# Converting float64 weights in place, without GpSimd, with later turns of gathered tokens and one conditional part

## The chip, the cores and the metric

The kernel runs on one core of a Trainium2 chip. Its engines are named as in the profile: PE (TensorE; PEld is its weight load), DVE (VectorE), ACT (ScalarE), POOL (GpSimd) and SP (SyncE, which here issues loads and stores). The metric is the device time of one execution in microseconds; of several runs the median is given.

## The reference, cut to what matters

Three parts follow each other: attention over chunks of 32 tokens with 8 memory keys, a dense feed-forward layer over 3072 tokens (model width 512, hidden 2048), and a routed layer in which each token goes to one of 8 experts (hidden 1024).

```python
for c in range(S // 32):                      # chunk attention, 4 x 8 heads, 768 tokens
    scores = q_c @ concat(mem_k, k_ctx).T / 8
    a = exp(scores - max); a = a / (sum + 1e-9)
    out[chunk] = a @ concat(mem_v, v_ctx)
h = x @ w_in                                  # dense layer, 512 -> 2048 -> 512
x = (h * sigmoid(h)) @ w_out
logits = x @ w_gate + modality_bias[modality_id]
e = argmax(logits); gate = softmax(logits)[e]
for each expert: out[mask] = gate[mask] * (relu(x[mask] @ w1[e]) @ w2[e])
```

The dense weights w_in and w_out reach the kernel as float64: two 32-bit words for each number.

## The kernel before

**Stages.** The 3072 tokens are taken in 8 blocks of 384. A block is four attention sub-blocks of 96 tokens, then 16 dense steps f of 128 hidden units, then the routing of its tokens. After the eight blocks come the expert tiles of 384 gathered tokens (two early ones, e0 and e1, six large ones, b0 to b5) and one small tile of 128 (s0). Block 0's dense steps run while the 16 pairs of weights (step f of w_in and of w_out, half 0 and half 1) are still being loaded and converted; later blocks use the converted pairs, which stay on chip.

**Products.** A product with full precision is three products of a reduced type, fp32r: high x high, high x low and low x high. So each weight is held as a high and a low part (tiles wh and wl), and so are the activations (xh and xl, gh and gl). `prod_h` (lines 469 to 475) makes the hidden units (tile hp), `prod_y` (477 to 482) the outputs (tile yp). Between them stand a tanh on ACT, `tanh_1` on DVE (508), a rounding copy on ACT (513, gh) and a subtraction on DVE (514, gl).

**Conversion** (lines 410 to 467) turns the two words of a float64 into a float32. The upper word has sign, exponent and the top of the mantissa, the lower word the rest. For both halves of a step:

- `load` (420, 422): two transfers of 512 KB, w_in as four pieces of 256 words per partition, w_out as 1024 words in one piece;
- `scale_down` (ACT, 429; DVE for step 0): the upper word, read as a float, times 2^-112, into tile wm;
- `shift` (DVE, 433): wm of both halves shifted left by 3, one instruction over 1024 words;
- `sign` (DVE, 437): the sign bit of the upper word is merged into wm;
- `rest` (ACT, 444, or DVE, 442, for the steps in `D_T1`): the lower word times 2^-29, into tile wt;
- `whole` (POOL, 448): wm = wm + wt as integers;
- `high` (ACT, 451): wh = wm rounded to fp32r;
- `low` (455): wl = wm - wh, on DVE for half 1 and on POOL for half 0.

**Attention.** Of a sub-block, `minima` (DVE, 355) reads the scores, `exps` (ACT, 362) makes the exponentials, `sums` (DVE, 367, 368) their reciprocal sums, `norm` (POOL, 373) scales two halves of four heads; then PE turns them (377), a copy (380) and the product with the values (385) follow, and the split into xh and xl (388, 391).

**Experts.** For each tile `ids` finds the tokens, `gather` (POOL, 843) fetches 128 rows from HBM by indirect DMA (tile xg), `turn` (PE, 849) transposes them into PSUM (xp), and ACT and DVE split them (852 and on). `put` (POOL, 1008) scatters results. The routing may need more tiles than the static ones: a seventh and further large tile, or a second and further small one. Each has a conditional part at the end (1037 to 1046), which loads a count into a register on all engines and skips the part where the count is not above 6 or 1.

**What sets the order.** All instructions are units of a planner (`Plan`): each has an engine, a cost in ns, a lag behind it (`extra`, the time of a transfer), the units that it waits for and its tiles. A list scheduler puts them in one static order per engine; nothing is reordered at run time. For a gather the lag is `DMA_LAG + 800` = 2700 ns; for a weight load 1900 ns. The load of step f waits for the last unit that reads the lower words of step f - 3. A list `first` fixes the order of the first loads.

```python
U(f"ga{x}", "Pool", 1040, lambda t=t: gather(t), [f"id{nm}/{gi}"], [f"xg{x}", f"gi{nm}"], extra=DMA_LAG + 800, **F)
U(f"tx{x}", "PE", 430, lambda t=t: turn(t), [f"ga{x}"], [f"xg{x}", f"xp{x}"], **F)
```

## Time and profile before

| | |
|---|---|
| median of 3 runs | 1007.29 us (1005.69 to 1008.43) |
| profiled execution | 1009.41 us |
| its span | 1007.6 us |
| mean granted TensorE clock, as a share of full | 0.972 |
| PE busy | 947.0 us (94%) |
| PEld busy | 834.9 us (83%) |
| DVE busy | 668.8 us (66%) |
| ACT busy | 442.4 us (44%) |
| POOL busy | 208.6 us (21%) |

Busy times are unions over one profiled execution, from the first to the last instruction; the execution's own time has 1.8 us more than the span. A share over the whole span is a mean over stages, so the stages are to be looked at one by one.

### The profile page before, as it was taken

What the parts mean: (1) busy time and instruction counts of PE and PEld (TensorE: products, weight loads), DVE (VectorE), ACT (ScalarE), POOL (GpSimd) and SP (SyncE); (2) the same over time, 40 slices, a digit from 0 to 9 for tenths busy, and PEclk for the clock granted to TensorE, in tenths of its full rate; (3) what the DMA queues carried; (4) which work ended last, traced back from release to release, by engine and by line L of the source; (5) the groups of instructions that cost most, each with busy time, mean ns of one, the idle gap of its engine ahead of it and who ended that gap; (6) DMA issues with size and microseconds to landing.
All of it is one profiled execution on the core that took longest, in us unless ns stands there. A gap on an engine that the chain in (4) does not pass through costs nothing. (4 is left out here: it accounts for less than half of the span.)

```text
span 1007.6 us, 16028 instructions
## 1 busy us (share of the span) xinstructions
PE 947.0 (94%) x5516; PEld 834.9 (83%) x5516; DVE 668.8 (66%) x1959; ACT 442.4 (44%) x1201; POOL 208.6 (21%) x174
## 2 busy tenths in 40 slices
PE   6687789999999999999999999999999999999994
...
GB/s 299 276 92 157 91 121 62 99 11 111 91 31 89 83 60 62 99 72 61 100 72 61 82 32 45 40 159 187 32 212 206 141 173 172 150 152 209 126 44 45
DMA packets 102402, 111.00 MB, mean 110 GB/s; under 512 B 22591, under 2 KB 76639, under 8 KB 102304
## 3 DMA queue, kind: packets, MB, share of 16 engines
...
q14 instruction: 51, 0.42, 0.1%
HBM read 97.20 MB, written 12.85 MB: 109 GB/s over the span
## 5 line engine op out<-in xcount | busy, mean ns | idle before, releaser
L373 POOL TENSOR_TENSOR pt<-pt,rs 96x512 f32<-96x512 f32 x64 | 80.6, 1278 | 416.3 <-DVE rs L368 340.4
L362 ACT ACTIVATE pt<-pt,mn 96x128 f32<-96x128 f32 x256 | 99.6, 391 | 27.9 <-DVE mn L355 27.7
L448 POOL TENSOR_TENSOR wm<-wm,wt 128x512 int32<-128x512 int32 x32 | 50.8, 1600 | 19.4 <-DVE wm L437 13.3
L362 ACT ACTIVATION_READ_ACCUMULATOR pt<-pt,mn 96x1 f32 x256 | 48.3, 189 | 0.0
L385 PE MATMUL pv<-px,v 128*64 128x96 f32 x512 | 30.8, 266 | 4.0 <-DVE mn L355 2.6
L385 PEld LDWEIGHTS pv<-px,v 128*64 128x64 f32 x512 | 24.6, 147 | 12.0 <-DVE mn L355 4.7
L455 POOL TENSOR_TENSOR wl<-wm,wh 128x512 fp32r<-128x512 f32 x16 | 24.7, 1544 | 4.5 <-ACT wh L451 4.5
L391 DVE TENSOR_TENSOR xl<-pv,xh 128x384 fp32r<-128x384 f32 x32 | 17.5, 547 | 11.8 <-ACT xh L388 11.8
L451 ACT CAST wh<-wm 128x512 fp32r<-128x512 f32 x32 | 19.6, 617 | 9.6 <-POOL wm L448 9.6
L388 ACT CAST xh<-pv 128x384 fp32r<-128x384 f32 x32 | 15.1, 473 | 18.4 <-PE pv L385 18.4
L455 DVE TENSOR_TENSOR wl<-wm,wh 128x512 fp32r<-128x512 f32 x16 | 21.1, 1321 | 1.3 <-ACT wh L451 1.3
L355 DVE DVE_READ_ACCUMULATOR2_ANT mn<- 96x1 f32 x256 | 20.1, 79 | 0.0
L433 DVE TENSOR_SCALAR wm<-wm 128x1024 int32<-128x1024 int32 x16 | 19.1, 1194 | 0.1
L843 POOL DMA_INDIRECT xge0.0_6891<-yd,gie x1 | 1.2, 1171 | 76.2 <-DMA rawxe0.1_6861<-in_moe_w_dram 76.2
L545 DVE DVE_READ_ACCUMULATOR2_ANT lg<- 128x1 f32 x192 | 15.5, 81 | 0.0
L367 DVE TENSOR_SCALAR rs<-sm 96x8 f32<-96x8 f32 x32 | 6.7, 210 | 1.8 <-ACT pt L362 1.8
L585 DVE TENSOR_SCALAR ya<-ya,rg 128x512 f32<-128x512 f32 x16 | 7.6, 481 | 0.0
L368 DVE RECIPROCAL rs<-rs 96x8 f32<-96x8 f32 x32 | 6.4, 199 | 1.1
L627 DVE TENSOR_SCALAR rej<-rows,rj 128x24 f32<-128x24 f32 x24 | 7.1, 294 | 0.0
L1008 POOL DMA_INDIRECT out_dram<-bye0.0_7456,sxe x1 | 1.0, 1024 | 28.4 <-ACT bye0.0_7456 L1005 28.4
L562 DVE TENSOR_SCALAR rw<-rd 128x24 f32<-128x24 f32 x8 | 5.6, 701 | 0.1
L474 PE MATMUL hp0.0_447<-xl,wh 128*128 128x384 f32 x4 | 1.6, 563 | 4.3 <-DVE xl L391 4.3
...
## 6 DMA issues: line engine op xcount, KB each, us to landing
...
wd0.0_100<-in_moe_w_in_dram SPq DMA_DIRECT2D x1, 512.0 KB
wd0.1_102<-in_moe_w_out_dram SPq DMA_DIRECT2D x1, 512.0 KB
wd1.0_152<-in_moe_w_in_dram SPq DMA_DIRECT2D x1, 512.0 KB
```

What stands on the lines that cost most here:

```text
L355: dve.tensor_tensor_reduce(out=T[f"pt{n}"][:, h, :], in0=T[f"sc{n}.{i // 2}"][:, h % 4, :], in1=mask, scale=-scale, scalar=3.0e38, op0=ALU ...
L362: act.activation(out=pt[:, h, :], in_=pt[:, h, :], func=AF.Exp, bias=T[f"mn{n}"][:, h:h + 1], scale=-1.0, accum_out=T[f"sm{n}"][:, h:h + 1])
L373: pool.tensor_tensor(out=pt[:, half, :], in0=pt[:, half, :], in1=bc(T[f"rs{n}"][:, half], [QB, 4, P]), op=ALU.mult)
L385: pe.matmul(T[f"pv{n}"][r:r + 64, h // 2, :], T[f"v{n}"][:, D * h:D * h + D], T[f"px{n}"][:, 4 * (h % 2) + h // 2, :], start=True, stop=True)
L388: act.copy(out=T[f"xh{j}"][:, :, cols], in_=T[f"pv{n}"])
L391: dve.tensor_tensor(out=T[f"xl{j}"][:, :, cols], in0=T[f"pv{n}"], in1=T[f"xh{j}"][:, :, cols].bitcast(F32), op=ALU.subtract)
L433: dve.tensor_scalar(out=mi, in0=mi, scalar1=3, scalar2=None, op0=ALU.logical_shift_left)
L448: pool.tensor_tensor(out=mi, in0=mi, in1=T[f"wt{f}"][:, i], op=ALU.add)
L451: (dve.tensor_copy if f in D_CH else act.copy)(out=T[f"wh{f}"][:, i], in_=T[f"wm{f}"][:, i])
L455: e.tensor_tensor(out=T[f"wl{f}"][:, i], in0=T[f"wm{f}"][:, i], in1=T[f"wh{f}"][:, i].bitcast(F32), op=ALU.subtract)
L545: dve.tensor_tensor_reduce(out=part(products), in0=part(y_at[t]), in1=T[f"wg{j}.{e // 2}"][:, e % 2], scale=1.0, scalar=0.0, op0=ALU.mult, ...
L585: dve.tensor_scalar(out=y, in0=y, scalar1=T[f"rg{j}"][:, t:t + 1], scalar2=None, op0=ALU.mult)
```

## The change

It has three parts, and a fourth that follows from the first.

1. *The conversion is done in place, and POOL has no part in it.* Tiles wm and wt are gone. The lower word is scaled where it stands (line 422 on DVE with a minimum of 7 for the steps in `D_T`; line 424 on ACT with a factor just under 2^-29), the sign is merged into it (428, DVE), the upper word is scaled where it stands (432, ACT), one instruction shifts the upper word left by 3 and merges the lower word into it by a bitwise or (436, DVE), the high part is rounded from it (439, ACT) and the low part is subtracted (442, DVE, both halves). So the integer addition becomes an or, and the shift has no instruction of its own.
2. *Gathers have a lag of 6500 ns in the plan* in the place of 2700.
3. *One conditional part* covers further large and further small tiles. The planning writes one number, the sum of two comparisons, in the place of two counts; the small list is planned behind the large one.
4. *Loads.* The host lays w_in and w_out out so that each half of a step is one piece of 4 KB per partition. Each half is a unit of its own, waits for the merge of its half three steps back, and has a place of its own in `first`.

```diff
+GATHER_LAG = 6500.0
...
-D_T1 = range(0, 16, 3)
-D_LO = [(f, 1) for f in range(16)]
-D_C1 = (0,)
-D_CH = ()
+D_T = range(0, 16, 3)
...
     def conversion(f):
         for i in range(2):
             T.new(f"wd{f}.{i}", "w", [P, DM, 2], I32)
-        T.new(f"wm{f}", "w", [P, 2, DM])
-        T.new(f"wt{f}", "w", [P, 2, DM], I32)
         T.new(f"wh{f}", "w", [P, 2, DM], F32R)
         T.new(f"wl{f}", "w", [P, 2, DM], F32R)
-        wd = [f"wd{f}.0", f"wd{f}.1"]
-
-        def load():
-            sp.dma_start(
-                out=T[wd[0]].rearrange("p (c f) w -> p c (f w)", c=KD), in_=w_in[:, f * P:f * P + P].bitcast(I32).rearrange("(c p) x -> p c x", p=P))
-            sp.dma_start(out=T[wd[1]].rearrange("p f w -> p (f w)"), in_=w_out[f * P:f * P + P, :].bitcast(I32))
-
-        def scale_down(i):
-            m, x = T[f"wm{f}"][:, i], T[wd[i]][:, :, 1].bitcast(F32)
-            if f in D_C1:
-                dve.tensor_scalar(out=m, in0=x, scalar1=2.0 ** -112, scalar2=None, op0=ALU.mult)
+
+        def load(i):
+            sp.dma_start(out=T[f"wd{f}.{i}"].rearrange("p f w -> p (f w)"), in_=(w_in, w_out)[i][f].bitcast(I32))
+
+        def rest(i):
+            x = T[f"wd{f}.{i}"][:, :, 0]
+            if f in D_T:
+                dve.tensor_scalar(out=x, in0=x.bitcast(U32), scalar1=2.0 ** -29, scalar2=7.0, op0=ALU.mult, op1=ALU.min)
             else:
-                act.activation(out=m, in_=x, func=AF.Copy, scale=2.0 ** -112)
-
-        def shift():
-            mi = T[f"wm{f}"].bitcast(I32)
-            dve.tensor_scalar(out=mi, in0=mi, scalar1=3, scalar2=None, op0=ALU.logical_shift_left)
+                act.activation(out=x, in_=x.bitcast(U32), func=AF.Copy, scale=7.49 * 2.0 ** -32)
 
         def sign(i):
-            mi = T[f"wm{f}"][:, i].bitcast(I32)
-            dve.scalar_tensor_tensor(out=mi, in0=T[wd[i]][:, :, 1], scalar=-2 ** 31, in1=mi, op0=ALU.bitwise_and, op1=ALU.bitwise_or)
-
-        def rest(i):
-            t, x = T[f"wt{f}"][:, i], T[wd[i]][:, :, 0].bitcast(U32)
-            if f in D_T1:
-                dve.tensor_scalar(out=t, in0=x, scalar1=2.0 ** -29, scalar2=None, op0=ALU.mult)
-            else:
-                act.activation(out=t, in_=x, func=AF.Copy, scale=2.0 ** -29)
+            x = T[f"wd{f}.{i}"]
+            dve.scalar_tensor_tensor(out=x[:, :, 0], in0=x[:, :, 1], scalar=-2 ** 31, in1=x[:, :, 0], op0=ALU.bitwise_and, op1=ALU.bitwise_or)
+
+        def exponent(i):
+            x = T[f"wd{f}.{i}"][:, :, 1].bitcast(F32)
+            act.activation(out=x, in_=x, func=AF.Copy, scale=2.0 ** -112)
 
         def whole(i):
-            mi = T[f"wm{f}"][:, i].bitcast(I32)
-            pool.tensor_tensor(out=mi, in0=mi, in1=T[f"wt{f}"][:, i], op=ALU.add)
+            x = T[f"wd{f}.{i}"]
+            dve.scalar_tensor_tensor(out=x[:, :, 1], in0=x[:, :, 1], scalar=3, in1=x[:, :, 0], op0=ALU.logical_shift_left, op1=ALU.bitwise_or)
 
         def high(i):
-            (dve.tensor_copy if f in D_CH else act.copy)(out=T[f"wh{f}"][:, i], in_=T[f"wm{f}"][:, i])
+            act.copy(out=T[f"wh{f}"][:, i], in_=T[f"wd{f}.{i}"][:, :, 1].bitcast(F32))
 
         def low(i):
-            e = dve if (f, i) in D_LO else pool
-            e.tensor_tensor(out=T[f"wl{f}"][:, i], in0=T[f"wm{f}"][:, i], in1=T[f"wh{f}"][:, i].bitcast(F32), op=ALU.subtract)
+            dve.tensor_tensor(out=T[f"wl{f}"][:, i], in0=T[f"wd{f}.{i}"][:, :, 1].bitcast(F32), in1=T[f"wh{f}"][:, i].bitcast(F32), op=ALU.subtract)
 
         C = dict(hop=CONV_SLACK)
-        U(f"c0_{f}", "SP", 2920, load, [f"cb_{f - CONV_AHEAD}.1" if f < KF - 2 else f"c5_{f - 2}.1", f"c0_{f - 1}"], wd, extra=DMA_LAG)
         for i in range(2):
-            U(f"c1_{f}.{i}", *(("DVE", 335) if f in D_C1 else ("ACT", 520)), lambda i=i: scale_down(i), [f"c0_{f}"], [wd[i], f"wm{f}"], **C)
-        U(f"ca_{f}", "DVE", 600, shift, [f"c1_{f}.0", f"c1_{f}.1"], [f"wm{f}"], **C)
-        for i in range(2):
-            U(f"cb_{f}.{i}", *(("DVE", 335) if f in D_T1 else ("ACT", 520)), lambda i=i: rest(i), [f"c0_{f}"], [wd[i], f"wt{f}"], **C)
-            U(f"cs_{f}.{i}", "DVE", 602, lambda i=i: sign(i), [f"ca_{f}"], [wd[i], f"wm{f}"], **C)
-            U(f"cl_{f}.{i}", "Pool", 1225, lambda i=i: whole(i), [f"cs_{f}.{i}", f"cb_{f}.{i}"], [f"wt{f}", f"wm{f}"], **C)
-            U(f"ch_{f}.{i}", *(("DVE", 335) if f in D_CH else ("ACT", 520)), lambda i=i: high(i), [f"cl_{f}.{i}"], [f"wm{f}", f"wh{f}"], **C)
-            U(f"c5_{f}.{i}", *(("DVE", 602) if (f, i) in D_LO else ("Pool", 1225)), lambda i=i: low(i), [f"ch_{f}.{i}"], [f"wm{f}", f"wh{f}", f"wl{f}"], **C)
+            x, wd = f"{f}.{i}", f"wd{f}.{i}"
+            U(f"c0_{x}", "SP", 400, lambda i=i: load(i), [f"cv_{f - CONV_AHEAD}.{i}", f"c0_{f}.0" if i else f"c0_{f - 1}.1"], [wd], extra=DMA_LAG)
+            U(f"cs_{x}", "DVE", 680, lambda i=i: sign(i), [f"ct_{x}"], [wd], **C)
+            U(f"c1_{x}", "ACT", 670, lambda i=i: exponent(i), [f"cs_{x}"], [wd], **C)
+            U(f"ct_{x}", *(("DVE", 420) if f in D_T else ("ACT", 660)), lambda i=i: rest(i), [f"c0_{x}"], [wd], **C)
+            U(f"cv_{x}", "DVE", 680, lambda i=i: whole(i), [f"c1_{x}", f"ct_{x}"], [wd], **C)
+            U(f"ch_{x}", "ACT", 640, lambda i=i: high(i), [f"cv_{x}"], [wd, f"wh{f}"], **C)
+            U(f"c5_{x}", "DVE", 680, lambda i=i: low(i), [f"ch_{x}"], [wd, f"wh{f}", f"wl{f}"], **C)
...
-        last = 1 + MAX_ST + E + (0 if move else 1)
-        dve.tensor_copy(out=ei[:, last:last + 1], in_=end[:, E - 1:E])
+        if move:
+            dve.tensor_scalar(out=T["plan"][:, DM - 1:DM], in0=end[:, E - 1:E], scalar1=float(N_BIG), scalar2=None, op0=ALU.is_gt)
+        else:
+            dve.scalar_tensor_tensor(out=ei[:, at + n:at + n + 1], in0=end[:, E - 1:E], scalar=float(N_SMALL), in1=T["plan"][:, DM - 1:DM], op0=ALU.is_gt, op1=ALU.add)
...
-        U_seq("plans", [100] * 9, lambda: plan_list("s"), ["pc"], ["plan", "plans"])
+        U_seq("plans", [100] * 9, lambda: plan_list("s"), ["pc", "planb"], ["plan", "plans"])
...
-            U(f"ga{x}", "Pool", 1040, lambda t=t: gather(t), [f"id{nm}/{gi}"], [f"xg{x}", f"gi{nm}"], extra=DMA_LAG + 800, **F)
+            U(f"ga{x}", "Pool", 1040, lambda t=t: gather(t), [f"id{nm}/{gi}"], [f"xg{x}", f"gi{nm}"], extra=GATHER_LAG, **F)
...
-        first = ["LQ0", "LK0", "mk", "LQ1", "LK1", "c0_0", "ident", "LV0", "c0_1", "LQ2", "LK2", "LV1", "c0_2", "LQ3", "LK3", "LV2", "c0_3", "LV3"]
+        first = ["LQ0", "LK0", "mk", "LQ1", "LK1", "c0_0.0", "c0_0.1", "ident", "LV0", "c0_1.0", "c0_1.1", "LQ2", "LK2", "LV1", "c0_2.0", "c0_2.1", "LQ3", "LK3", "LV2", "c0_3.0", "c0_3.1", "LV3"]
...
-        for nm, n0, n1, col in (("b", N_BIG, MAX_ST, at), ("s", N_SMALL, E, at + 1)):
-            cnt = nc.values_load(
-                ei[0:1, col:col + 1], min_val=0, max_val=n1,
-                skip_runtime_bounds_check_because="a count of tiles that the number of tokens and experts bounds")
-            with tc.If(cnt > n0):
-                T.restart()
-                chain.clear()
-                begin.clear()
-                experts([(nm, i) for i in range(n0, n1)])
-                T.emit()
+        more = nc.values_load(
+            ei[0:1, at:at + 1], min_val=0, max_val=2,
+            skip_runtime_bounds_check_because="a sum of two results of comparisons")
+        with tc.If(more > 0):
+            T.restart()
+            chain.clear()
+            begin.clear()
+            experts([("b", i) for i in range(N_BIG, MAX_ST)] + [("s", i) for i in range(N_SMALL, E)])
+            T.emit()
...
+    if name == "moe_w_in":
+        return a.reshape(-1, P, a.shape[1] // P, P).transpose(2, 1, 0, 3).reshape(-1, P, a.shape[0])
+    if name == "moe_w_out":
+        return a.reshape(-1, P, a.shape[1])
```

The lines of the changed kernel are lower by 3 near the attention (line 355 becomes 352, 373 becomes 370), 508 becomes 494, 514 becomes 500, 474 becomes 460, 480 to 482 become 466 to 468, and 849 becomes 837.

How it moves instructions is shown at three places. The first is SP's queue at the start, rows 5 to 16 of the program on SP: mk is the masks, wd the weights (step, half), qk and v the attention's inputs of sub-blocks 1 to 3 in turn. Before:

```order
L272 DMA mk<-in_const_dram 96x3x128
L420 DMA wd0.0_100<-in_moe_w_in_dram 128x4x256
L422 DMA wd0.1_102<-in_moe_w_out_dram 128x1024
L344 DMA v_119<-in_v_dram 128x512
L285 DMA ident<-in_const_dram 128x128
L338 DMA qk_139<-in_q_dram 128x4x96
L341 DMA qk_139<-in_k_dram 128x4x128
L420 DMA wd1.0_152<-in_moe_w_in_dram 128x4x256
L422 DMA wd1.1_154<-in_moe_w_out_dram 128x1024
L344 DMA v_192<-in_v_dram 128x512
L338 DMA qk_206<-in_q_dram 128x4x96
L341 DMA qk_206<-in_k_dram 128x4x128
```

With the change:

```order
L269 DMA mk<-in_const_dram 96x3x128
L417 DMA wd0.0_100<-in_moe_w_in_dram 128x1024
L341 DMA v_102<-in_v_dram 128x512
L282 DMA ident<-in_const_dram 128x128
L335 DMA qk_115<-in_q_dram 128x4x96
L338 DMA qk_115<-in_k_dram 128x4x128
L417 DMA wd0.1_119<-in_moe_w_out_dram 128x1024
L341 DMA v_123<-in_v_dram 128x512
L335 DMA qk_130<-in_q_dram 128x4x96
L338 DMA qk_130<-in_k_dram 128x4x128
L417 DMA wd1.0_152<-in_moe_w_in_dram 128x1024
L341 DMA v_157<-in_v_dram 128x512
```

The v, q and k loads of sub-blocks 2 and 3 now stand ahead of weights that they stood behind, and w_out of step 0 stands behind six more of the small loads.

The second place is DVE in block 0's dense steps, around the subtractions gl0.2 and gl0.3 (t is the hidden half's other step, wl the low part of a weight, rs the attention's sums). Before:

```order
L442 TENSOR_SCALAR wt_589<-wd6.0_504 128x512
L508 SCALAR_TENSOR_TENSOR t0.2_586<-t0.2_586,hp0.2_540 128x384
L455 TENSOR_TENSOR wl_582<-wm_438,wh_556 128x512
L442 TENSOR_SCALAR wt_589<-wd6.1_506 128x512
L514 TENSOR_TENSOR gl0.2_613<-t0.2_586,gh0.2_609 128x384
L433 TENSOR_SCALAR wm_592<-wm_592 128x1024
L437 SCALAR_TENSOR_TENSOR wm_592<-wd6.0_504,wm_592 128x512
L437 SCALAR_TENSOR_TENSOR wm_592<-wd6.1_506,wm_592 128x512
L508 SCALAR_TENSOR_TENSOR t0.3_633<-t0.3_633,hp0.3_595 128x384
L455 TENSOR_TENSOR wl_631<-wm_510,wh_616 128x512
L514 TENSOR_TENSOR gl0.3_663<-t0.3_633,gh0.3_659 128x384
```

With the change:

```order
L436 SCALAR_TENSOR_TENSOR wd4.0_415<-wd4.0_415 128x512
L442 TENSOR_TENSOR wl_520<-wd3.1_383,wh_478 128x512
L428 SCALAR_TENSOR_TENSOR wd4.1_425<-wd4.1_425 128x512
L494 SCALAR_TENSOR_TENSOR t0.2_528<-t0.2_528,hp0.2_503 128x384
L428 SCALAR_TENSOR_TENSOR wd5.0_446<-wd5.0_446 128x512
L436 SCALAR_TENSOR_TENSOR wd4.1_425<-wd4.1_425 128x512
L500 TENSOR_TENSOR gl0.2_565<-t0.2_528,gh0.2_561 128x384
L442 TENSOR_TENSOR wl_568<-wd4.0_415,wh_540 128x512
L442 TENSOR_TENSOR wl_568<-wd4.1_425,wh_540 128x512
L436 SCALAR_TENSOR_TENSOR wd5.0_446<-wd5.0_446 128x512
L428 SCALAR_TENSOR_TENSOR wd5.1_470<-wd5.1_470 128x512
L494 SCALAR_TENSOR_TENSOR t0.3_581<-t0.3_581,hp0.3_546 128x384
```

The scaling (442), the shift (433) and the two sign merges (437) are gone; between the same hidden steps stand sign merges (428), merges with the shift (436) and two subtractions per step (442).

The third place is PE in expert tile b0, where the tokens of tile b1 are turned (xp is the turned tile, hp and yp the products of a step). Before:

```order
L480 MATMUL ypb0.2_7850<-ehxb0.1_7629,ghxb0.1_7860 128x512
L481 MATMUL ypb0.2_7850<-elxb0.1_7651,ghxb0.1_7860 128x512
L482 MATMUL ypb0.2_7850<-ehxb0.1_7629,glxb0.1_7867 128x512
L849 MATMUL xpb1.0_7925<-ident,xgb1.0_7845 128x128 x4
L849 MATMUL xpb1.1_7931<-ident,xgb1.1_7869 128x128 x4
L849 MATMUL xpb1.2_7936<-ident,xgb1.2_7889 128x128 x4
L474 MATMUL hpxb0.3_7943<-xhb_7770,ehxb0.3_7664 128x384 x4
L474 MATMUL hpxb0.3_7943<-xlb_7778,ehxb0.3_7664 128x384 x4
L474 MATMUL hpxb0.3_7943<-xhb_7770,elxb0.3_7706 128x384 x4
L480 MATMUL ypb0.0_7848<-ehxb0.2_7653,ghxb0.2_7904 128x512
```

With the change:

```order
L460 MATMUL hpxb0.3_7877<-xhb_7717,ehxb0.3_7625 128x384 x4
L460 MATMUL hpxb0.3_7877<-xlb_7730,ehxb0.3_7625 128x384 x4
L460 MATMUL hpxb0.3_7877<-xhb_7717,elxb0.3_7663 128x384 x4
L837 MATMUL xpb1.0_7891<-ident,xgb1.0_7796 128x128 x4
L466 MATMUL ypb0.0_7800<-ehxb0.2_7611,ghxb0.2_7859 128x512
L467 MATMUL ypb0.0_7800<-elxb0.2_7637,ghxb0.2_7859 128x512
L468 MATMUL ypb0.0_7800<-ehxb0.2_7611,glxb0.2_7872 128x512
L466 MATMUL ypb0.1_7801<-ehxb0.2_7611,ghxb0.2_7859 128x512
...
L468 MATMUL ypb0.2_7802<-ehxb0.2_7611,glxb0.2_7872 128x512
L837 MATMUL xpb1.1_7921<-ident,xgb1.1_7814 128x128 x4
L837 MATMUL xpb1.2_7926<-ident,xgb1.2_7826 128x128 x4
L460 MATMUL hpxb0.4_7932<-xhb_7717,ehxb0.4_7763 128x384 x4
```

The first turn has moved behind the hidden product of step 3, and the second and third behind the nine output products of step 2.

## Rows read from the trace of the kernel before

**Rows 1.** The page, PE in 40 slices of 25.2 us, busy tenths.

```profile
PE   6687789999999999999999999999999999999994
```

**Rows 2.** Timeline of PE: start us, us, engine, line, out<-in, [idle before].

```profile
41.69 0.69 PE L474 MATMUL hp0.0_447<-xl,wh 128*128 128x384 f32 x1 [4.26 <-DVE xl L391]
...
148.96 0.51 PE L474 MATMUL hp1.0_1463<-xh,wh 128*128 128x384 f32 x2
```

**Rows 3.** Windows: length; PE, PEld, DVE, ACT, POOL busy (x); PE clock, DMA share, GB/s.

```profile
0.00:41.60 41.60, 26.33 (x188) 19.76 (x188) 29.76 (x103) 26.43 (x88) 21.73 (x20) 0.64 0.87 269
41.60:149.00 107.40, 84.97 (x484) 70.89 (x485) 101.78 (x195) 69.69 (x187) 76.75 (x57) 0.93 0.42 139
149.00:227.40 78.40, 78.40 (x503) 69.24 (x501) 51.41 (x175) 30.97 (x95) 8.19 (x8) 1.00 0.17 55
```

**Rows 4.** Timeline of DVE, 57 to 69 us.

```profile
57.18 0.68 DVE L437 SCALAR_TENSOR_TENSOR wm<-wd5.0_440,wm 128x512 int32<-128x512 int32 x1
57.78 0.68 DVE L437 SCALAR_TENSOR_TENSOR wm<-wd5.1_442,wm 128x512 int32<-128x512 int32 x1
...
61.53 0.41 DVE L442 TENSOR_SCALAR wt<-wd6.1_506 128x512 int32<-128x512 uint32 x1
61.87 0.55 DVE L514 TENSOR_TENSOR gl0.2_613<-t0.2_586,gh0.2_609 128x384 fp32r<-128x384 f32 x1
...
67.06 1.62 DVE L514 TENSOR_TENSOR gl0.3_663<-t0.3_633,gh0.3_659 128x384 fp32r<-128x384 f32 x1
```

**Rows 5.** The page, costliest groups: busy us, mean ns | idle before.

```profile
L373 POOL TENSOR_TENSOR pt<-pt,rs 96x512 f32<-96x512 f32 x64 | 80.6, 1278 | 416.3 <-DVE rs L368 340.4
...
L448 POOL TENSOR_TENSOR wm<-wm,wt 128x512 int32<-128x512 int32 x32 | 50.8, 1600 | 19.4 <-DVE wm L437 13.3
...
L455 POOL TENSOR_TENSOR wl<-wm,wh 128x512 fp32r<-128x512 f32 x16 | 24.7, 1544 | 4.5 <-ACT wh L451 4.5
...
L455 DVE TENSOR_TENSOR wl<-wm,wh 128x512 fp32r<-128x512 f32 x16 | 21.1, 1321 | 1.3 <-ACT wh L451 1.3
...
L433 DVE TENSOR_SCALAR wm<-wm 128x1024 int32<-128x1024 int32 x16 | 19.1, 1194 | 0.1
```

**Rows 6.** Timeline of POOL, 64.91 us.

```profile
64.91 3.35 POOL L448 TENSOR_TENSOR wm<-wm,wt 128x512 int32<-128x512 int32 x2 [1.36 <-DVE wm L437]
```

**Rows 7.** List of PE's waits: us in total, times, longest us.

```profile
PE sc2.0_174 L350 <- DVE wm L433: 3.7, 1, 3.7
...
PE xpb5.2_9300 L849 <- DMA xgb5.2_9253<-yd,gib: 2.4, 1, 2.4
...
PE hpxb0.0_7783 L474 <- ACT xhb L852: 0.7, 1, 0.7
...
PE xpb2.2_8277 L849 <- DMA xgb2.2_8230<-yd,gib: 0.6, 1, 0.6
```

**Rows 8.** Lines 1037 and 1124: ns min/median/max, first and last start.

```profile
L1037 POOLq TENSOR_LOAD <-ei x2: 311/406/502, 994.7 to 1000.6; - x2
...
L1124 POOLq DRAIN  x3: 40/107/4148, 1002.7 to 1007.4; - x3
```

**Rows 9.** Windows of one DVE line each: L437, L442, L514 in turn.

```profile
0.00:149.00 149.00, 31.36 (x32) 0.85 0.55 175
...
0.00:149.00 149.00, 11.37 (x12) 0.85 0.55 175
...
0.00:149.00 149.00, 15.50 (x16) 0.85 0.55 175
```

**Rows 10.** Timeline of DVE at the start.

```profile
7.44 0.36 DVE L287 CAST masks<-mk 96x384 bf16<-96x384 f32 x1 [6.30 <-DMA mk<-in_const_dram]
...
12.28 0.42 DVE L442 TENSOR_SCALAR wt<-wd0.1_102 128x512 int32<-128x512 uint32 x1
```

**Rows 11.** DMA issues: KB each, us to landing.

```profile
wd2.1_225<-in_moe_w_out_dram SPq DMA_DIRECT2D x1, 512.0 KB, 8.0
```

**Rows 12.** Window of the matmuls of line 474, 691 to 994 us.

```profile
691.00:994.00 303.00, 147.51 (x768) 137.31 (x768) 0.99 0.43 140
```

5 lines of the change are left out of this document (2 added, 3 removed).

## Prediction

> **What bounds the kernel now.** I read the page's slices first. TensorE (PE) is busy nine tenths or more in 33 of the 40 slices, all of them behind the sixth [rows 1]: in that part only PE's own work or its waits can give time back. In the first six slices (25.2 us each) PE has gaps. PE's timeline gives the ends of the stage: the first dense product (hp0.0) starts at 41.69 us, the first product of block 1 (hp1.0) at 148.96 [rows 2]. Windows cut there show what is full [rows 3]: from 41.6 to 149.0 us PE is busy 85.0 of 107.4 us, ScalarE (ACT) 69.7, VectorE (DVE) 101.8, so DVE bounds the first 149 us; after it PE is busy 78.4 of 78.4 us at a granted clock of 1.00, and DVE is not the limit. The reader should see two regimes: what the conversion costs DVE is paid in full before 149 us, and nothing it does matters after that.
>
> Why is DVE so full? Its conversion instructions take far longer than they need. Two sign merges in a row start 0.60 us apart, and a scalar instruction over 512 strided words lets the next start after 0.34 us [rows 4]. But line 455 on DVE averages 1.32 us and line 433 1.19 us [rows 5], and the subtraction of gl0.3 took 1.62 us where that of gl0.2 took 0.55 [rows 4]. The timeline of GpSimd (POOL) has two integer additions (line 448) ending at 68.26 us; gl0.3 started at 67.06 and ended at 68.68, 0.42 us after them [rows 6]. DVE stood still while POOL worked. POOL has 32 additions (50.8 us) and 16 subtractions (24.7 us) of the conversion in this stage [rows 5], so such meetings are the rule.
>
> The last two views are small. In PE's list of waits, seven gathered tiles (e0.0, e0.1, b1.2 to b5.2) hold their turn for between 2.4 us (b5.2) and 0.6 (b2.2), 7.7 us in all [rows 7]. At the end, POOL passes two conditional parts: line 1037's load occurs twice, the second at 1000.6, and the final drain follows at 1002.7 [rows 8].
>
> **The change, part by part.**
>
> *Conversion, DVE.* Removed in the stage: 32 merges of line 437 (31.4 us), 12 scalings of line 442 (11.4 us) [rows 9], 16 subtractions of line 455 (21.1 us) and 16 shifts of line 433 (19.1 us) [rows 5]: 83.0 us. Added: 32 sign merges, 32 merges with the shift, 32 subtractions, each over 512 elements with two operands, priced at the 0.60 us from start to start [rows 4]: 57.6 us; and 12 scalings at 0.34: 4.1 us. Together 61.7, a saving of 21.3 us. The 16 subtractions for the dense hidden half (line 514) take 15.5 us now [rows 9]; freed of POOL's conversion they should take 0.55 each, 8.8 us, a saving of 6.7.
>
> *What still blocks.* POOL keeps the normalizations (line 373, 1.28 us each [rows 5]), 18 in this stage. They cost DVE nothing if they fall beside the PSUM-reading minima, and at most their whole length, 18 x 1.28 = 23 us. I take 0.5 us each, 9 us, nearer the middle because DVE's instructions that meet them are now shorter and more frequent. DVE's busy time before 149 us is 29.8 + 101.8 = 131.5 us [rows 3]; it becomes 131.5 - 21.3 - 6.7 + 9 = 112.5 us.
>
> *Conversion, ACT.* 82 conversion instructions become 84 (two scalings of step 0 come over from DVE); ACT has 37.7 us idle in the second window [rows 3], so two more cost nothing. Their cover is that idle time; were it gone, they would cost some 1.3 us. The in-place order is new: scaling of the low word, sign, exponent on ACT, merge, rounding on ACT, subtraction. Each half now passes between ACT and DVE up to five times and both queues run in order, so an ACT instruction that waits for DVE holds the exponentials behind it.
>
> *Start.* DVE's first work was the mask at 7.44 us; now its first instruction needs w_in step 0, which lands after the mask and before 12.28 us, when DVE read the next load without a wait [rows 10]. I take 10 us: 2.5 us later. Against that, the loads of sub-blocks 2 and 3 stand ahead of 0.5 and 1.5 MB of weights in the queue. The scores of sub-block 2 waited 3.7 us [rows 7]; the releaser named there is a conversion on which they don't depend, so I read it as the landing of their K. I let this gain stand as reserve and count only the loss.
>
> *Loads.* A weight load now waits for the merge three steps back instead of the scaling. Three steps last some 20 us (3 x 107.4 / 16 [rows 3]), and a load took 8.0 to land [rows 11]: hidden. If not, SP's queue holds the next q, k and v loads behind it and the stage grows by one landing, 8 us.
>
> *Sum of the stage.* DVE is idle 149 - 131.5 = 17.5 us now. I add 2.5 for the start and 5 for the hand-overs (bounds: nothing, and the 19 us that would eat the whole saving). 112.5 + 25 = 137.5 us, 11.5 us earlier. PE needs 26.3 + 85.0 = 111.3 us of it and ACT 96.1, so both fit.
>
> *Gathered turns.* The planner's gather lag moves each group by one product for the first tile and two for the others. The 768 matmuls of line 474 in the expert stage take 147.5 us [rows 12], 0.19 each, so 12 of them, one product, 2.3 us. The longest wait, 2.4 us, is of a third tile, which moves by 4.6, so all 7.7 us go. The turn of e0.2 now stands one product ahead of its user; the nearest row is the 0.7 us that block b0 waits after its turns [rows 7], which I halve: 7.4 us. Block b0's own turns don't move and keep their waits. Bounds: 0 and 7.7.
>
> *One conditional part.* POOL's second pass, from 1000.6 to the drain at 1002.7, goes: 2.1 us. The bounds are nothing (if the longer skip costs as much) and 2.1. The extra planning step on DVE lies under PE's work.
>
> Sum: 11.5 + 7.4 + 2.1 = 21.0 us. The rows are of an execution of 1009.4 us (span 1007.6), 2.1 above the median of 1007.3; I take the saving from the median: **986 us**.
>
> **The rivals.**
>
> *PE takes over (chance 0.16).* If the norms hardly block and the hand-overs overlap, DVE needs 103.5 + 17.5 = 121 us, and PE's 111.3 us plus its start sets the end near 125: 24 us less. 1007.3 - 24 - 9.5 = 974 us. For it: ACT's slack. Against: half of PE's waits in the second window are for the hidden half's two DVE steps, which stay.
>
> *The chain of hand-overs eats the stage (0.14).* In two in-order queues every misplaced link stops both engines. At 1.2 us lost per step, 16 steps take back the saving: only the other two parts remain, 1007.3 - 9.5 = 998 us. For it: five crossings per half where there were three or fewer on these two engines. Against: the stages of several halves stand interleaved in the new order.
>
> *In-place writes are slow (0.04), slower.* All 64 merges now write every second word. Rows show strided reads at full pace (the sign merge, 0.60), never a strided write. If it doubled the merge, DVE gets 64 x 0.6 = 38 us more and the end is 986 + 38 = 1024 us. It decides from 21 / 64 = 0.33 us extra each, 0.93 instead of 0.60. The Trainium skill, SBUF — State Buffer, in its note on cachelines under the DMA port swizzle, says that accesses keep full rate while at least two fall on one 16-byte line; two words of this step do. No run here shows a strided write yet; by the rule this rival falls, and I leave it little.
>
> *DVE was the wrong place (0.03), slower too.* Suppose the long instructions are DVE's own. The 76 that go average 83.0 / 76 = 1.09 us; 96 at that price and 12 scalings are 109 us, 26 more than now, so the stage ends near 175 + 2.5 and the whole at about 1007 + 28 - 9.5 = 1026 us. The Trainium skill, Perfetto Trace Analysis, Optimizing Scalar/DVE Operations, advises moving work off a saturated DVE, to Scalar or even GPSIMD, though it adds that the shared port may spoil the latter. The change goes the other way with DVE at 95% of the window. The rows at 0.60 and 0.55 beside idle POOL speak against this rival.
>
> *It doesn't do what it says (0.05).* The turns or the skip gain nothing and the stage only a little: within 0.3% of now. A taken conditional part would cost far more, but the comparisons are those of before, whose trace holds no seventh large and no second small expert tile.
>
> **How the numbers follow.** My forecast with its bounds (978 to 994) has 0.58. The others: 974 (0.16), 998 (0.14), no change (0.05), slower (0.07). A difference of 0.3%, 3 us, is about what a measurement of this kernel can tell from none. Faster: 0.58 + 0.16 + 0.14 = 0.88; same 0.05; slower 0.07. The range takes in the first three cases with a margin of 3 to 4 us for the unknown norm and wait costs, 970 to 1001 us, and leaves out some 0.15.
>
> **What would show it.** Right: lines 436 and 428 near 0.68 us busy with 0.60 from start to start; line 500 near 0.55; POOL under 30 us before block 1; the first product of block 1 at 137 us (125 to 145); no wait of PE for a gathered tile but b0's; a single line for the conditional on POOL. Wrong: merges above 0.9 us; line 500 still near 1 us with only norms on POOL; ACT idle before its conversion lines while DVE is idle too (the chain); block 1's first product later than 149 us; or a new wait of e0's first product for ACT above 1 us.

## The result, and the profile after

The changed kernel takes **980.2 us** (median of 4 runs, 977.8 to 982.5) against 1006.9 us before: a ratio of 0.973, 95% interval 0.971 to 0.976, or 26.7 us less. The forecast was 986 us, from 970 to 1001. By stages of the profiled executions (1009.41 us before, 979.85 after):

| us | before | forecast | after |
|---|---|---|---|
| start to first product of block 1 | 149.0 | 137.5 | 135.0 |
| from there to the end of PE's last matmul | 845.1 | 837.7 | 832.2 |
| behind PE's last matmul | 13.6 | 11.5 | 10.8 |

The ends are read from PE's timeline: the first product of block 1 and the last matmul of the changed kernel,

```profile
134.97 0.52 PE L460 MATMUL hp1.0_1411<-xh,wh 128*128 128x384 f32 x2
...
966.78 0.39 PE L962 MATMUL yps0.0_9855<-ehxs0.1.3_9777,ggxs0.1_9852 128*128 128x512 f32 x1
```

and the last matmul of the kernel before, which answers to the second row ([rows 2] answer to the first):

```profile
993.65 0.39 PE L974 MATMUL yps0.0_9903<-ehxs0.1.3_9825,ggxs0.1_9900 128*128 128x512 f32 x1
```

The slices (24.5 us each now; PE, tenths, [rows 1]) reach nine tenths in the fourth, fall to eight in the fifth, and stay at nine from the sixth to the last but one:

```profile
PE   6789899999999999999999999999999999999995
```

The windows of the changed kernel, in the columns of [rows 3], show where the stage's time went. To 135.0 us DVE is busy 111.2 us where it was 131.5 to 149 us, ACT 98.6 where it was 96.1, and POOL 26.0 where it was 98.5:

```profile
0.00:35.90 35.90, 25.56 (x185) 19.07 (x185) 19.81 (x96) 20.17 (x78) 8.31 (x12) 0.62 0.74 239
35.90:135.00 99.10, 84.89 (x488) 71.30 (x489) 91.34 (x229) 78.41 (x198) 17.70 (x14) 0.93 0.51 174
0.00:135.00 135.00, 110.45 (x672) 90.37 (x673) 111.15 (x324) 98.58 (x275) 26.02 (x26) 0.85 0.57 191
```

Windows of one DVE line each (428, 436, 442, 422, 500, in turn) answer to [rows 9] and the DVE groups of [rows 5]:

```profile
0.00:135.00 135.00, 21.55 (x32) 0.85 0.57 191
...
0.00:135.00 135.00, 23.23 (x32) 0.85 0.57 191
...
0.00:135.00 135.00, 22.87 (x32) 0.85 0.57 191
...
0.00:135.00 135.00, 4.91 (x12) 0.85 0.57 191
...
0.00:135.00 135.00, 9.98 (x16) 0.85 0.57 191
```

The four conversion lines are 72.6 us busy, and the hidden half's subtraction (500) 10.0 us in the place of 15.5. On the timeline of DVE two merges with the shift, which write every second word in place, start 0.61 us apart, and gl0.0 takes 0.55, the pace of [rows 4]:

```profile
36.44 0.69 DVE L436 SCALAR_TENSOR_TENSOR wd1.0_152<-wd1.0_152 128x512 int32<-128x512 int32 x1
37.05 0.69 DVE L436 SCALAR_TENSOR_TENSOR wd1.1_185<-wd1.1_185 128x512 int32<-128x512 int32 x1
...
45.92 0.55 DVE L500 TENSOR_TENSOR gl0.0_476<-t0.0_463,gh0.0_472 128x384 fp32r<-128x384 f32 x1
```

In PE's list of waits no gathered tile is left. Two rows of it: the second scores wait for DVE, which stands before w_in of step 0, and block b0's first product waits as in [rows 7]:

```profile
PE sc1.1_140 L347 <- DVE mn L352: 4.1, 1, 4.1
...
PE hpxb0.0_7735 L460 <- ACT xhb L840: 0.7, 1, 0.7
```

At the end there is one pass of POOL over the conditional part, and the drain stands 5.1 us behind its load, where the drain of [rows 8] stood 8.0 us behind the first of two loads:

```profile
L1024 POOLq TENSOR_LOAD <-ei x1: 497/497/497, 967.9 to 967.9; - x1
...
L1115 POOLq DRAIN  x3: 40/107/4148, 973.0 to 977.7; - x3
```

### The profile page after: what moved, and what is told of

Read it like the earlier page. It is cut to its first block, busy times and chain, and to the rows that moved or that the text cites. A ratio compares the mean times of both kernels' runs of the same rounds, so it can differ in the third digit from the quotient of the medians.

```text
span 978.0 us, 15961 instructions
## 1 busy us (share of the span) xinstructions
PE 941.7 (96%) x5516; PEld 832.0 (85%) x5516; DVE 647.7 (66%) x1989; ACT 444.6 (45%) x1203; POOL 141.3 (14%) x126
## 5 line engine op out<-in xcount | busy, mean ns | idle before, releaser
L370 POOL TENSOR_TENSOR pt<-pt,rs 96x512 f32<-96x512 f32 x64 | 83.0, 1316 | 497.9 <-DVE rs L365 391.6
L359 ACT ACTIVATE pt<-pt,mn 96x128 f32<-96x128 f32 x256 | 99.5, 391 | 13.6 <-DVE mn L352 13.3
L382 PEld LDWEIGHTS pv<-px,v 128*64 128x64 f32 x512 | 24.5, 146 | 10.2 <-issue 2.6
L531 DVE DVE_READ_ACCUMULATOR2_ANT lg<- 128x1 f32 x192 | 15.6, 82 | 0.0
L347 PE MATMUL sc1.1_140<-qk 64*96 64x128 f32 x8 | 2.0, 428 | 4.1 <-DVE mn L352 4.1
L550 DVE TENSOR_TENSOR rw<-rw,rows 128x24 f32<-128x24 f32 x8 | 5.4, 675 | 0.3
L261 PE MATMUL warm<-zeros 128*128 128x512 bf16 x8 | 3.3, 591 | 1.2 <-DVE zeros L263 1.2
```

Source lines behind the costliest of these rows:

```text
L359: act.activation(out=pt[:, h, :], in_=pt[:, h, :], func=AF.Exp, bias=T[f"mn{n}"][:, h:h + 1], scale=-1.0, accum_out=T[f"sm{n}"][:, h:h + 1])
L370: pool.tensor_tensor(out=pt[:, half, :], in0=pt[:, half, :], in1=bc(T[f"rs{n}"][:, half], [QB, 4, P]), op=ALU.mult)
L382: pe.matmul(T[f"pv{n}"][r:r + 64, h // 2, :], T[f"v{n}"][:, D * h:D * h + D], T[f"px{n}"][:, 4 * (h % 2) + h // 2, :], start=True, stop=True)
L531: dve.tensor_tensor_reduce(out=part(products), in0=part(y_at[t]), in1=T[f"wg{j}.{e // 2}"][:, e % 2], scale=1.0, scalar=0.0, op0=ALU.mult, ...
```

## The experiments

The theory of the prediction: DVE bounds the early stage because it stands still while POOL works; taking POOL out of the conversion and shortening DVE's share frees it. The rivals there: DVE's own work is what counts; the chain of hand-overs eats the gain. The spread of the stage first, since many readings hang on it.

**The changed kernel once more.**

> The changed kernel once more, unchanged, beside the three others of this set, to see how far the end of the stage moves between executions of one kernel (135.0 us in its first profile, 137.3 with the earlier turns, which don't touch the stage). Both theories below need this spread: expected 135 to 138 us and a time of 978 to 983.

980.4 us (5 runs, 978.4 to 981.2; ratio to before 0.972, 0.970 to 0.974). The stage ended at 136.6 us (first profile 135.0; 137.3 in a later run that leaves the stage as it is). So one profile places the stage within some 2 us, and smaller differences below need the times.

### Does DVE stand still while POOL works?

The tile dz and its clearing on POOL at the start belong to it as well.

```diff
+        def idle_add(i):
+            pool.tensor_tensor(out=dz, in0=T[f"wl{f}"][:, i].bitcast(I32), in1=dz, op=ALU.add)
...
+            U(f"dm_{x}", "Pool", 1, lambda i=i: idle_add(i), [f"c5_{x}", "dz"], [f"wl{f}"])
```

> The changed kernel with 32 additions on POOL that nobody waits for: each adds a finished low part of the weights into a tile of its own (128 x 512 int32, two operands, as the addition of the kernel before), and its result is not used. The order on all other engines is that of the changed kernel. Theory (DVE stands while POOL works on such operands): the 16 normalizations left in the stage cost DVE some 7 us, 0.43 each; an addition before the change ran 1.6 us. So DVE loses between 0.4 and 1.0 us for each of the 32, its lines 428, 436, 442 and 500 grow from 0.60 and 0.47 us start to start, and the first product of block 1 comes at 148 to 167 us instead of 135. Rival (the long instructions before were DVE's own, or waits for data): nothing depends on the additions, so lines and stage stay within 1 us of the changed kernel.

The first product of block 1 came at 154.3 us, 19.4 later, and the time, of a single run, was 998.7. The page's group of the additions and the window of the stage:

```profile
L447 POOL TENSOR_TENSOR dz<-wl,dz 128x512 int32<-128x512 int32 x32 | 53.3, 1665 | 41.6 <-DVE wl L444 38.3
```

```profile
0.00:154.30 154.30, 116.53 (x671) 91.65 (x672) 137.51 (x324) 100.02 (x274) 80.82 (x59) 0.85 0.50 169
```

DVE has the same instructions in the same order and is busy 137.5 us in the place of 111.2: 26.4 us, or 0.82 for each of the 32 additions, with nothing waiting for their results. POOL's normalizations do stand behind them in its queue, but a wait for those would show as idle time of DVE, and that is 16.8 us here and 23.8 in the changed kernel. One place on the two timelines, POOL first, DVE second:

```profile
59.10 3.32 POOL L447 TENSOR_TENSOR dz<-wl,dz 128x512 int32<-128x512 int32 x2 [2.37 <-DVE wl L444]
```

```profile
57.81 0.55 DVE L506 TENSOR_TENSOR gl0.2_575<-t0.2_536,gh0.2_571 128x384 fp32r<-128x384 f32 x1
58.28 0.68 DVE L444 TENSOR_TENSOR wl<-wd4.0_417,wh 128x512 fp32r<-128x512 f32 x1
58.88 0.68 DVE L444 TENSOR_TENSOR wl<-wd4.1_428,wh 128x512 fp32r<-128x512 f32 x1
59.48 1.79 DVE L438 SCALAR_TENSOR_TENSOR wd5.0_451<-wd5.0_451 128x512 int32<-128x512 int32 x1
61.19 1.78 DVE L430 SCALAR_TENSOR_TENSOR wd5.1_476<-wd5.1_476 128x512 int32<-128x512 int32 x1
```

POOL's two additions run from 59.10 to 62.42 us. The low parts before them (58.28, 58.88) start 0.60 apart; the merge that starts at 59.48 takes 1.79 us, the next 1.78. The theory holds: the long instructions of [rows 5] were not DVE's own.

Which instructions stand still is to be seen in the kernel before as well. Line 508, whose one operand is in PSUM, has 16 instructions in the stage that take 0.54 us each, beside a POOL that is busy two thirds of it; by the timelines 14 of the 16 lie over an instruction of POOL (the window of that line):

```profile
0.00:149.00 149.00, 8.70 (x16) 0.85 0.55 175
```

The Trainium skill, SBUF — State Buffer, Who interferes with whom, says that a DVE instruction with two inputs in SBUF contends with a GpSimd instruction that reads SBUF, and one with at most one such input, outside the modes that use two ports, does not. The trace agrees in both: merges of two SBUF operands go from 0.68 to 1.8 us, line 508 stays at 0.54.

One operand in SBUF is not enough to be spared, though: of the long instructions in the kernel before, the shift (433) and the scalings (442) have a single one. Line 442 takes 0.41 us where POOL is idle [rows 4], and 1.51 over a subtraction of POOL that runs from 102.28 to 104.02 us:

```profile
102.79 1.51 DVE L442 TENSOR_SCALAR wt<-wd12.1_918 128x512 int32<-128x512 uint32 x1
```

Both lines pass their words faster than the merges do: 1024 in 0.60 us from start to start where nothing holds line 433, 512 in 0.34 for line 442, against 512 in 0.60 for a merge. Whether that is a mode of two ports, no run here shows.

**One operation given back to POOL.**

```diff
-            dve.tensor_tensor(out=T[f"wl{f}"][:, i], in0=T[f"wd{f}.{i}"][:, :, 1].bitcast(F32), in1=T[f"wh{f}"][:, i].bitcast(F32), op=ALU.subtract)
+            (dve if i else pool).tensor_tensor(out=T[f"wl{f}"][:, i], in0=T[f"wd{f}.{i}"][:, :, 1].bitcast(F32), in1=T[f"wh{f}"][:, i].bitcast(F32), op=ALU.subtract)
...
-            U(f"c5_{x}", "DVE", 680, lambda i=i: low(i), [f"ch_{x}"], [wd, f"wh{f}", f"wl{f}"], **C)
+            U(f"c5_{x}", *(("DVE", 680) if i else ("Pool", 1225)), lambda i=i: low(i), [f"ch_{x}"], [wd, f"wh{f}", f"wl{f}"], **C)
```

> The changed kernel with one operation given back to POOL: the low part of half 0 (16 subtractions in the stage). It takes 16 x 0.60 = 9.6 us of work off DVE, which bounds the stage. Theory (DVE stands while POOL works): the 16 subtractions of about 1.5 us on POOL cost DVE 0.4 to 1.0 us each, 6 to 16 us, and each low part arrives about 1 us later, so nothing is won: first product of block 1 at 133 to 142 us, time 978 to 987. Rival (work off the bound engine is time won): stage 9 us shorter, first product of block 1 at 126 us, time 971.

983.8 us (4 runs, 983.2 to 984.2; ratio 0.976, 0.974 to 0.979), all of them above the changed kernel's, by 3.5 us in the medians (3 to 4.5 by the ratios to the kernel before). The windows of the stage and of line 442 (DVE, then POOL):

```profile
0.00:139.40 139.40, 113.43 (x672) 93.41 (x673) 116.57 (x310) 99.14 (x277) 47.10 (x44) 0.84 0.55 187
```

```profile
0.00:139.40 139.40, 13.91 (x16) 25.29 (x16) 0.84 0.55 187
```

DVE lost 16 subtractions, 9.6 us at 0.60, and is busy 116.6 us in the place of 111.2: POOL's 16 cost the others 15.0 us, 0.94 each. The theory holds again, and the rival (work off the bound engine is time won) has the wrong sign. The Trainium skill, Perfetto Trace Analysis, Optimizing Scalar/DVE Operations, advises to move work off a saturated DVE and doubts it for GpSimd, because of the shared port; the runs show the doubt right: 3 to 4.5 us slower.

### What of the conversion brought the 14 us?

**POOL out, nothing else.** For the or, the lower words are scaled as in the changed kernel.

```diff
-D_LO = [(f, 1) for f in range(16)]
+D_LO = [(f, i) for f in range(16) for i in range(2)]
...
-            pool.tensor_tensor(out=mi, in0=mi, in1=T[f"wt{f}"][:, i], op=ALU.add)
+            dve.tensor_tensor(out=mi, in0=mi, in1=T[f"wt{f}"][:, i], op=ALU.bitwise_or)
...
-            U(f"cl_{f}.{i}", "Pool", 1225, lambda i=i: whole(i), [f"cs_{f}.{i}", f"cb_{f}.{i}"], [f"wt{f}", f"wm{f}"], **C)
+            U(f"cl_{f}.{i}", "DVE", 602, lambda i=i: whole(i), [f"cs_{f}.{i}", f"cb_{f}.{i}"], [f"wt{f}", f"wm{f}"], **C)
```

> The kernel before with POOL taken out of the conversion and nothing else: same tiles, same loads, shift and sign merge as before; the 32 whole-word additions become 32 bitwise ors on DVE (the lower words scaled as in the changed kernel) and all 32 low parts are on DVE. DVE gets 48 instructions more, 28.8 us of work at 0.60. Theory (the lock by POOL was the cost): conversion on DVE takes 16 x 0.56 + 96 x 0.60 + 4 = 71 us against some 78 us now, line 514 falls to 0.47 us, and the stage ends at 142 to 147 us; then taking POOL out gave about a third of the 14 us, and the rest is the merged shift and the order of the loads. Rival (DVE is the bound and gets 28.8 us more): first product of block 1 at 165 to 178 us. Second rival (all 14 us come from POOL): 135 to 137 us.

994.4 us (4 runs, 991.8 to 996.1; ratio 0.988, 0.985 to 0.990), and the stage ended at 134.3 us:

```profile
0.00:134.30 134.30, 109.68 (x672) 87.33 (x672) 121.57 (x340) 95.19 (x267) 27.16 (x26) 0.89 0.60 194
```

The second rival is what happened, and my theory of a third was wrong: with 48 instructions more on DVE (28.8 us) and no merged shift, DVE is busy 121.6 us, ten less than before, and the whole 14 us are there.

**All three parts of the change, with the old chain on separate tiles.** The edits are those above with the gather lag and the single conditional part.

> The changed kernel with the old conversion on separate tiles, POOL out of it: shift and sign merge as before, the whole word by a bitwise or on DVE, all low parts on DVE; loads and their layout as before, later turns, one conditional part. DVE has 16 shifts more than in the changed kernel, 10 us of work by the two traces. Theory (the in-place chain gives its saving back in hand-overs and in the split loads): stage 133 to 136 us as with POOL taken out alone, time 979 to 983, the same as the changed kernel within 2 us and 2 to 5 above the one with joined loads. Rival (DVE's work sets the stage): 10 us later than the changed kernel, 145 us and 990.

980.5 us (5 runs, 978.7 to 980.7; ratio 0.972, 0.970 to 0.974): the changed kernel's time. Its stage, cut at 36 us, about where the dense steps begin, and below it that of the changed kernel's second profile:

```profile
0.00:36.00 36.00, 25.56 (x184) 18.87 (x184) 24.00 (x100) 22.46 (x82) 10.78 (x12) 0.87 0.87 268
36.00:135.80 99.80, 87.45 (x487) 71.87 (x488) 98.09 (x241) 73.58 (x190) 16.37 (x14) 0.93 0.50 165
```

```profile
0.00:36.00 36.00, 26.84 (x188) 20.06 (x189) 20.43 (x97) 20.83 (x79) 8.31 (x12) 1.00 0.74 239
36.00:136.60 100.60, 86.19 (x485) 72.66 (x485) 90.77 (x228) 77.60 (x196) 17.72 (x14) 0.90 0.50 172
```

DVE has 10.9 us more to do and the stage ends no later. What the change saves on DVE beyond POOL comes back as DVE's idle time: 13.7 us here (12.0 before 36 us and 1.7 behind), 25.4 there (15.6 and 9.8). With the old chain DVE is busy 98.1 of 99.8 us behind 36 us, so there it still is the limit; with the change it is busy nine tenths. But two things differ between these kernels, the chain and the loads, and the next runs part them.

**The loads.** First both halves of a step as one unit again, in the old order of the first loads:

```diff
...
+        U(f"c0_{f}", "SP", 2920, load, [f"cv_{f - CONV_AHEAD}.0", f"cv_{f - CONV_AHEAD}.1", f"c0_{f - 1}"], [f"wd{f}.0", f"wd{f}.1"], extra=DMA_LAG)
...
-            U(f"c0_{x}", "SP", 400, lambda i=i: load(i), [f"cv_{f - CONV_AHEAD}.{i}", f"c0_{f}.0" if i else f"c0_{f - 1}.1"], [wd], extra=DMA_LAG)
...
```

> The changed kernel with the loads issued as before: both halves of a step as one unit of the plan, behind the merges of both halves three steps back, with the first loads in the order of the kernel before; the layout in memory stays the new one. The prediction counted 2.5 us lost at the start and left the earlier K of sub-blocks 2 and 3 as reserve; measured, the first dense step had its last operand at 38.99 us against 41.69. Theory (the order of the first loads gave these 2.7 us): first dense product complete near 41.5 us, first product of block 1 at 137 to 139 us, time 2 to 4 us above the changed kernel. Rival (the stage is set by DVE's work and the start is hidden): block 1 at 134 to 136 us, no difference in the time.

978.4 us (4 runs, 975.1 to 978.5; ratio 0.971, 0.969 to 0.974) and a stage of 130.3 us, so the theory fell, and its rival too: the split loads seem to cost time, 1.8 us by these medians. It was run again beside the changed kernel:

> The kernel with joined loads once more, unchanged, beside the changed kernel on the same chip. Its first profile ended the stage at 130.35 us, 4.6 before the changed kernel, but its time was only 1.8 below. Theory (splitting the loads and their new first order cost about 4 us): stage 129 to 132 us, time 2 to 5 us below the changed kernel. Rival (the 4.6 us were chance): stage 133 to 137, same time within 1 us.

977.5 us (5 runs, 977.2 to 979.2; ratio 0.970, 0.968 to 0.972), stage 132.8 us. The time fits the theory, 2.9 us below the changed kernel beside it; the stage lies between theory and rival. Third, the load's wait put back as well:

```diff
-        U(f"c0_{f}", "SP", 2920, load, [f"cv_{f - CONV_AHEAD}.0", f"cv_{f - CONV_AHEAD}.1", f"c0_{f - 1}"], [f"wd{f}.0", f"wd{f}.1"], extra=DMA_LAG)
+        U(f"c0_{f}", "SP", 2920, load, [f"ct_{f - CONV_AHEAD}.1" if f < KF - 2 else f"c5_{f - 2}.1", f"c0_{f - 1}"], [f"wd{f}.0", f"wd{f}.1"], extra=DMA_LAG)
```

> The kernel with joined loads, and each load waiting for the scaling of the lower words three steps back, as in the kernel before, in the place of the merge. In SP's order the loads of steps 3 to 5 then stand ahead of the q and k loads of sub-blocks 4 to 6; in the changed kernel the load of step 4 was issued at 36.1 us and ACT waited 2.3 us for it, before it was issued at 23.3 us. Theory (the later wait is a cost that the prediction set at nothing): stage 126 to 130 us, 1 to 4 us below the kernel with joined loads. Rival (the wait is hidden behind DVE's and ACT's work on steps 0 to 3): 130 to 132 us, no difference.

976.4 us (5 runs, 974.6 to 977.8; ratio 0.969, 0.967 to 0.971), stage 129.8 us. The windows of the stage of the three, in the order told, the last two cut at 36 us:

```profile
0.00:130.30 130.30, 105.50 (x671) 84.86 (x672) 111.20 (x324) 99.55 (x274) 28.81 (x26) 0.91 0.59 198
```

```profile
0.00:36.00 36.00, 24.93 (x190) 18.71 (x191) 23.98 (x101) 23.47 (x83) 10.26 (x12) 0.70 0.79 250
36.00:132.80 96.80, 85.19 (x484) 71.09 (x483) 87.50 (x224) 76.46 (x194) 18.57 (x14) 0.92 0.50 173
```

```profile
0.00:36.00 36.00, 24.35 (x196) 18.63 (x197) 24.59 (x102) 23.44 (x82) 9.84 (x12) 0.76 0.84 273
36.00:129.80 93.80, 82.42 (x478) 68.12 (x478) 87.20 (x223) 75.97 (x193) 17.94 (x14) 0.95 0.49 169
```

DVE's work is the same 111 to 112 us in all; only its idle time differs, and the windows show where.

*The chain.* The old chain has joined loads too. Beside it the in-place chain with joined loads takes 3.0 us less in the set that ran together (977.5 and 980.5), and with the load's wait of the old chain as well 4.1 less (976.4, all five runs below all five); the layout of the weights in memory still differs. So of the 10.3 to 10.6 us of work that the chain saves on DVE, 3 to 4 reach the end. The rest comes back behind 36 us, where DVE is idle for 9.3 and 6.6 us in the place of 1.7. In DVE's list of waits there, those of conversion lines are the smaller part, 1.6 and 0.4 us; more stands before the last step of the hidden half and the minima of sub-blocks 5 and 6.

*The loads.* Splitting them takes the gain away again (980.4), and this loss lies before 36 us: there DVE is idle for 16.1 and 15.6 us in the changed kernel's two profiles, and for 12.0 and 11.4 with joined loads, as with the old chain (12.0).

All five runs of the last kernel lie below all five of the changed kernel beside it, by 4 us in the medians, so it beats the changed kernel, though the intervals of the two ratios (0.967 to 0.971 and 0.970 to 0.974) just meet. Of its two steps the joined loads are 2.9 us in the set that ran together and the wait 1.1; the second alone is within the spread. With split loads ACT waits for the load of step 4, by 2.3 to 2.9 us in three executions (list of ACT's waits, the first profile), and the first hidden product of step 2 starts at 49.7 us. With joined loads this wait is 0.5 us or nothing, and the product starts at 42.8 and 41.3 us in the last two kernels:

```profile
ACT wd4.0_415 L424 <- DMA wd4.0_415<-in_moe_w_in_dram: 2.3, 1, 2.3
```

**The masks first.**

```diff
-        U("masks", "DVE", 270, lambda: dve.tensor_copy(out=masks, in_=T["mk"]), ["mk"], ["mk"])
+        U("masks", "DVE", 270, lambda: dve.tensor_copy(out=masks, in_=T["mk"]), ["mk"], ["mk"], boost=9.0e5)
...
-        C = dict(hop=CONV_SLACK)
+        C = dict(hop=CONV_SLACK, boost=-40000.0 if f == 0 else 0.0)
```

> The changed kernel with the masks and the first minima ahead of the conversion of step 0 on DVE and ACT (a higher rank for the masks, a lower one for step 0's conversion). In the changed kernel DVE's first work waits 8.7 us for w_in of step 0, the masks stand behind it, and PE waits 4.1 us in the second scores. Theory: the minima start at about 7.5 us, the scores wait less than 1 us, and the stage ends 1 to 3 us earlier, 132 to 134 us, time 977 to 979. Rival (step 0's weights become the last operand of the first product, as the conversion now starts later): the first product waits longer for its low part and the stage ends at 135 to 138 us.

980.9 us (4 runs, 979.6 to 981.9; ratio 0.974, 0.972 to 0.977), stage 134.7 us: no gain, so the theory fell, and the second scores still wait 1.7 us for DVE. The planner answered by setting sub-block 4 ahead of the dense steps, and PE stood 11.1 us for its normalization; the first dense product came at 46.1 us, ten later:

```profile
45.48 0.90 PE L374 MATMUL xp4.0_457<-ident,pt 96*128 96x96 f32 x4 [11.06 <-POOL pt L370]
46.09 1.63 PE L460 MATMUL hp0.0_464<-xh,wh 128*128 128x384 f32 x4
```

And still the stage ended at the same time. A late first product is no loss in itself here; what stands before it is work that the stage has to do anyway. But as the order changed with the masks, this run does not tell what DVE's late start costs.

### The two small parts

**Later turns alone.**

```diff
+GATHER_LAG = 6500.0
...
-            U(f"ga{x}", "Pool", 1040, lambda t=t: gather(t), [f"id{nm}/{gi}"], [f"xg{x}", f"gi{nm}"], extra=DMA_LAG + 800, **F)
+            U(f"ga{x}", "Pool", 1040, lambda t=t: gather(t), [f"id{nm}/{gi}"], [f"xg{x}", f"gi{nm}"], extra=GATHER_LAG, **F)
```

> The kernel before with the planned lag of the gathers alone raised to 6500 ns. In the two traces the stretch from the first product of block 1 to PE's last matmul is 845.0 us before and 832.2 after, 12.9 us less, where the prediction had 7.4. Theory: all of it comes from the later turns, the waits themselves (8.5 us) and the slow clock and restarts that follow them. Then the first product of block 1 stays at 149 us, the stretch is 832 to 833 us, the end behind PE stays at 13.6 us, and the time is 12 to 13 us below the kernel before. Rival: only the waits go and 4 us come from something else of the change (the earlier stage, the planning): then 836 to 838 us for the stretch and 7 to 9 us less in the time.

996.6 us (4 runs, 996.1 to 997.0; ratio 0.989, 0.986 to 0.991): 11.2 us less. Stage 148.5 us, stretch 832.4, end 14.0. The theory holds in the stretch; the time is 0.8 us short of what it named. In its list of PE's waits one row of the expert stage is left from [rows 7]:

```profile
PE hpxb0.0_7783 L475 <- ACT xhb L853: 0.8, 1, 0.8
```

**The changed kernel with the old lag.**

```diff
-GATHER_LAG = 6500.0
+GATHER_LAG = 2700.0
```

> The changed kernel with the planned lag of the gathers put back to 2700 ns. If the three parts add up, the stage stays at 135 us, the end at 10.8 us, the stretch between is back at 845 us, and the time is 12 to 13 us above the changed kernel, 992 to 994 us. If the 2.4 us wait of b5.2 and the slow clock behind it (4.3 us together) were a chance of that one execution, the stretch is about 841 us and the time near 989. If the prediction's 7.4 us was right and the rest came from elsewhere, 839 to 840 us and 987.

993.4 us (4 runs, 988.3 to 995.8; ratio 0.985, 0.982 to 0.989), 13 us above the changed kernel; in the profiled execution the stretch was 842.0 us: the time fits the first case, the stretch lies nearer the second. The parts add up within the spread, which is wide here. One reason is on the timelines of PE at b5.2. The kernel before:

```profile
922.40 0.63 PE L849 MATMUL xpb5.2_9300<-ident,xgb5.2_9253 128*128 128x128 f32 x4 [2.40 <-DMA xgb5.2_9253<-yd,gib]
922.78 1.46 PE L474 MATMUL hpxb4.3_9307<-xhb,ehxb4.3_9136 128*128 128x384 f32 x4
924.04 1.48 PE L474 MATMUL hpxb4.3_9307<-xlb,ehxb4.3_9136 128*128 128x384 f32 x4
```

and this one:

```profile
909.23 0.63 PE L837 MATMUL xpb5.2_9252<-ident,xgb5.2_9205 128*128 128x128 f32 x4 [2.41 <-DMA xgb5.2_9205<-yd,gib]
909.61 0.96 PE L460 MATMUL hpxb4.3_9259<-xhb,ehxb4.3_9088 128*128 128x384 f32 x4
910.41 0.87 PE L460 MATMUL hpxb4.3_9259<-xlb,ehxb4.3_9088 128*128 128x384 f32 x4
```

Both waited 2.4 us. In the first execution groups of four matmuls then took 1.46 and 1.48 us, in the second 0.96 and 0.87. The windows around them (the clock is the column behind POOL's) have a granted clock of 0.83, a mean between its two levels of 1.2 and 2.4 GHz, and of 1.00:

```profile
920.00:930.00 10.00, 7.60 (x34) 7.25 (x35) 3.78 (x6) 2.77 (x6) 1.22 (x2) 0.83 0.72 264
```

```profile
905.00:915.00 10.00, 7.59 (x45) 6.79 (x44) 5.01 (x8) 3.60 (x7) 1.00 (x1) 1.00 0.87 304
```

The three groups took 3.7 us from the first start to the next line (926.51 in the kernel before) where they take 2.1 in the changed kernel (896.53 to 898.61). So a wait can cost its length, or some 1.6 us more. Of two further executions one had slow matmuls behind this wait (one conditional part alone, 3.2 us), one none (POOL out, 2.5 us).

**One conditional part alone.** The edit is the hunk on `more` with the two lines of the planning.

> The kernel before with the single conditional part alone (and its sum of two comparisons in the planning). Theory: the end behind PE's last matmul goes from 13.6 to 10.8 us as in the changed kernel, all else stays: 149 us for the stage, 845 us for the stretch, and 2 to 3 us less in the time. Rival: the end depends on when the last scatter lands and the skip is hidden under it; then the end stays within 0.5 us of 13.6 and the time does not move. Second rival: the longer part to skip costs more than the one saved; then the end is longer than 13.6.

1005.6 us (12 runs, 1003.5 to 1007.6; ratio 0.998, 0.996 to 0.999): 2.2 us less. Lines 1038 and 1125 on POOL answer to [rows 8]:

```profile
L1038 POOLq TENSOR_LOAD <-ei x1: 497/497/497, 994.6 to 994.6; - x1
...
L1125 POOLq DRAIN  x3: 40/107/4148, 999.2 to 1003.9; - x3
```

The stage (149.1 us) and the stretch (844.9) did not move, the end is 10.2 us. The theory holds; both rivals fall.

## Why the prediction was right, and where not

**The time and the side.** 980.2 us lies in the range and near the forecast; the saving is 26.7 us where 21.0 were forecast. All three terms came out larger, the turns most of all. The likeliest case, DVE freed of POOL, is the one that the runs show. Alone, POOL out gives 13.9 us, the turns 11.2, the conditional part 2.2: 27.3 us, where the changed kernel has 26.7 to 27.7. Nothing is left for the in-place chain with split loads taken together; apart, they are 3 to 4 us each, of opposite sign and each near the spread. The marks named beforehand came: lines 428 and 436 are 0.67 and 0.73 us busy on the mean, line 500 0.62 (0.55 where nothing holds it), POOL 26 us, no gathered tile is waited for, and POOL passes one conditional part.

**What still blocks.** The normalizations were priced at 0.5 us each, 9 us. From start to start the four lines with two SBUF operands take 6.7 us more than at 0.60 and 0.47 (lines 428, 436 and 442: 62.5 us for 96; line 500: 9.3 for 16). The guess was of the right size.

**Sum of the stage: right in sum, wrong in part of the cause.** DVE busy was forecast at 112.5 us and is 111.2, by errors that cancel. The 83.0 us removed are busy times, in which neighbours overlap by 0.08 us, while the 61.7 added go from start to start; counted so, the lines removed took 78.2, and their saving was 4.8 us too large. Against that, 0.7 us more came from line 514, the blocking was 2.3 below its 9, and three small lines that the sum left out gave 3.2 (367 and 303, which POOL had held too, and 427, which went). DVE idle was forecast at 25 us and is 23.8: 16.1 before 36 us, 7.8 behind.

The step that was wrong in its cause is the one that takes every DVE saving off the stage's end alike, less 5 us for the hand-overs and 2.5 for the start. Taking POOL out is worth the whole 14 us. Of the 10 us that the merged shift and the in-place words save beyond it, 3 to 4 reached the end with joined loads and none with split ones. The rival that the hand-overs eat the gain, at 0.14, was half true: DVE's idle time behind 36 us ate most of what the shorter work brought (5 to 8 us with joined loads), not what the freed engine brought. DVE's waits in conversion lines, the hand-overs in the narrow sense, are 0.4 to 1.6 us of it; that the rest follows from them is argued, not shown.

**Start: right in place, a little small.** I set 2.5 us of loss and called the earlier K a reserve. DVE starts at 9.8 us in the place of 7.4, and before 36 us it is idle for 16 us with split loads and 11 to 12 in the kernels with joined ones. That is about the whole 3 to 4 us by which the kernels with joined loads are faster in the set that ran together; PE's wait for the K of sub-block 2 (3.7 us) is gone, as supposed, but DVE's idle time shows no gain from it. **Loads**, set at nothing as hidden, are not quite hidden: ACT waits 2.3 us for step 4. But that wait ends at 41.5 us, and between 36 and 50 us DVE is idle for 1.4 and 1.8 us with split loads and for 0.6 to 0.9 with joined ones, so it holds the smaller part of the loss. The larger part belongs to the first loads; whether to their split or to their order, no run here tells.

**Gathered turns: mis-sized.** 7.4 us forecast, 12.7 in the stretch and 11.2 in the time. The direction and the list of tiles were right. Left out were the slow matmuls after b5.2 (some 1.6 us in that execution), what stands behind each wait besides, and that b0's tiles gain too. In two other executions with the old lag and no slow matmuls after b5.2 (POOL out; the changed kernel with the old lag) nine turns wait 7.2 us in all and the stretch is 9.3 and 9.8 us longer than with later turns: some 0.25 us more for each wait. Of b0 the turns stand where they stood, as the prediction said, but the larger lag moves the gathers ahead. Relative to the first product of e0, b0's first gather is issued at 60.7 us in the place of 63.3.

**One conditional part** was forecast at 2.1 us and gives 2.2; the profiled ends differ by 2.8. **Strided writes** and **DVE the wrong place** fell: merges start 0.60 us apart in place, and moving work to POOL costs time. The Trainium skill, SBUF — State Buffer, in its note on cachelines, gives full rate where at least two accesses fall on one 16-byte line; the trace agrees, at 0.60.

Open: what sets the stage's end at 130 to 137 us now. PE is busy 105 to 113 us, DVE 111 to 112, ACT 98 to 100. Behind 36 us DVE is the fullest, nine tenths and more, but none is full, and no kernel here takes away a single wait of the chain.
